# An SSM convolution and a linear-attention block: single named PSUM banks, 512-column pieces and 32-row tiles

## The chip, the cores and the metric

The kernel runs on one core of a Trainium2 chip. The engines work side by side, each through its own queue in order: PE (TensorE: matmuls, with weight loads shown as PEld), DVE (VectorE), ACT (ScalarE), POOL (GpSimd) and SP (SyncE, which here only issues DMAs). They meet through semaphores. Matmuls write PSUM, 8 banks of 512 float32 columns on 128 partitions; DVE and ACT copy results from there to SBUF. The metric is the device time of one execution in microseconds (us), lower is better.

## The reference

Two independent blocks, their outputs side by side. S = 2048 tokens, D = 576 channels, 32 heads of 18, all bf16.

```python
def _A_ref(q, k, v, shift_k, ssm_k, ssm_D):
    ...
    for t in range(ks):                                   # ks = 4
        k_shift = k_shift + k_pad[:, t:t + S, :] * shift_k[:, ks - 1 - t][None, None, :]
    kv = k_shift * v
    ...                                                   # y: causal convolution of kv with ssm_k,
    y_f = kv_f * kf_f[None, :, :, :]                      # over S, by FFTs of length 2 S
    ...
    y = y + kv * ssm_D[None, None, :]
    return q * y

def _B_ref(x, wqkv, wo):
    ...                                                   # q, k, v = x @ wqkv, per head
    phi = lambda t: jnp.where(t > 0, t + 1, jnp.exp(t)) + 1e-6
    pq, pk = phi(q), phi(k)
    kv = jnp.einsum("bhsd,bhse->bhde", pk, v)
    z = jnp.einsum("bhsd->bhd", pk)
    num = jnp.einsum("bhqd,bhde->bhqe", pq, kv)
    den = jnp.einsum("bhqd,bhd->bhq", pq, z)[..., None] + 1e-6
    o = num / den
    return (lambda x, *d: x.transpose(*d))(o, 0, 2, 1, 3).reshape(B, S, D) @ wo
```

## The kernel before

Everything is one list of small work units, `ORDER` (L30), written out by hand. A unit's name picks a function (`UNITS`, L667), its numbers are arguments, a last letter is the engine of its copy out of PSUM (A: ACT, D: DVE; P: POOL, for products and convolution steps). `tc.manual_schedule()` issues the units in that order, and each engine's queue, SP's too, takes its instructions in that order.

Block A works on channel chunks `ACH` (four of 128, then one of 64), for the input u = kv and the kernel h:
- `cv` (L413): shift convolution and product with v, in four stages of elementwise steps over [128, 16 x 128], each on DVE or POOL. The shift weights stand copied to all partitions in `Wj`, from a DMA that writes them 128 times (L338) and one ACT copy (L342). k, v, q come in by groups of chunks, `GRP`: 256, 256 and 64 channels.
- `hT` (L436): 16 PE transposes of h. `h1`/`u1` (L451): stage one of the transform, 8 matmuls of 128 columns with `G[ri]` as weights (cosines and sines, from `_dft_index`, L131, and `_sine`, L209); one call for each half `bg` and each `ri`, copied to `Ch`/`Cu`.
- `ht`/`ut` (L464): DMA transposes to `Ct`. `h2`/`u2` (L472): stage two, 8 matmuls of 512 columns on 64-row, 32-column tiles, to `T` (h) and `SU` (u).
- `pX`, `pT` (L487): the spectra's products, on DVE.
- `i1` (L497): the first inverse stage, 32 matmuls of 128 columns on two 64-row tiles with `W` as the moving operand; four calls for each 128-channel chunk (`hf`, `z`), each with a copy of 1024 columns to `V`.
- `i2` (L513): the last inverse stage with `F`, the transposes of `G` (`FT`, L524); DVE multiplies by q out of PSUM. `st` stores.

Block B:
- `xd`: x transposed by DMA. `k` (L392): one block of 128 rows, 5 matmuls of 512 and 5 of 64 columns; `q` (L401): channel groups `HCH` of 126 in pairs. Both go through `phi` (L387): exp on ACT, then min and max on DVE.
- `G` (L564): x^T pk with ones columns that carry eps, 16 matmuls of 512 and 16 of 65 columns for each block of features; DVE takes a column (`ex`), ACT adds it in its copy. `kv` (L576), `M` (L597): weights combined with the output projection. `den` (L605): denominators and reciprocals, as rows 32 j + head.
- `bc` (L630): 1/den spread to the heads' channels by a matmul with a 0/1 matrix `esel` (built on POOL at L94 and masked four times by `es` on DVE, L623), then a DVE multiply into `pqT`; 2 matmuls of 512 columns a call, 10 calls.
- `o` (L640): 10 matmuls for 128 rows, copied by ACT, stored by one DMA of 144 KB.

PSUM is a pool of four slots of two banks (L257), given out in turn to every unit.

Of the kernel before, what the change touches and what calls it, by code (L numbers as in the profile page):

```python
# [16 lines left out]
S = 2048  # L17
# [9 lines left out]
ACH = [(0, 128), (128, 128), (256, 128), (384, 128), (512, 64)]  # L27
# [3 lines left out]
wm io wu.0 ix.0 sin.1 id ix.1 hl.0 iw wk wu.40 sin.0 hT.0.D FT.1.D h1.0.0.0.A h1.0.1.0.A FT.0.D h1.0.1.1.A  # L31
h1.0.0.1.A iv sw W lw.0 xd.2 q.2.0 hc lw.1 k.8 q.2.2 q.2.1 ls Wj hl.1 hT.1.D k.9 k.11 k.10 h1.1.1.0.D xd.0 k.3
kl.0 cv.0.0.D one h1.1.0.0.A k.1 ht.0.0 h2.0.0.0.A h2.0.0.1.A eps cv.0.1.DD cv.0.2.DD q.0.1 h1.1.1.1.A q.0.0
h1.1.0.1.A xd.3 q.3.0 q.0.2 vl.0 cv.0.3.PDD k.2 cv.1.0.P k.0 ht.0.1 h2.0.1.1.A q.3.1 k.12 u1.0.1.1.A k.15
h2.0.1.0.D ht.1.1 h2.1.1.0.A k.13 u1.0.0.1.A hl.2 hT.2.D u1.0.0.0.A cv.1.1.PD k.14 xd.1 u1.0.1.0.A xl.2
cv.1.2.DD cv.1.3.DPP ht.1.0 xl.1 h2.1.1.1.A q.1.1 h2.1.0.1.A h2.1.0.0.A q.1.0 q.1.2 h1.2.1.0.A ut.0.1 k.7
u2.0.1.0.D u2.0.1.1.A k.6 h1.2.0.1.A k.4 ut.0.0 u2.0.0.1.D u2.0.0.0.A k.5 pX.0.0 pT.0.0 u1.1.1.0.A u1.1.1.1.A
q.3.2 u1.1.0.1.A xl.0 xl.3 kl.1 pX.0.1 pT.0.1 u1.1.0.0.A es G.0 vl.1 h1.2.0.0.A h1.2.1.1.A cv.2.0.D cv.2.1.DD
cv.2.2.DD G.2 ut.1.0 G.4 u2.1.0.1.D u2.1.0.0.A ut.1.1 i1.0.0.1.A hl.3 i1.0.0.0.A i1.0.1.1.A i1.0.1.0.A
cv.2.3.DDD ql.0 cv.3.0.D cv.3.1.DD u2.1.1.1.A ht.2.0 u2.1.1.0.A pX.1.1 pT.1.1 hT.3.A G.1 lwv pX.1.0 pT.1.0  # L40
h2.2.0.1.A ht.2.1 G.3 cv.3.2.DD u1.2.0.0.A i2.0.0 kl.2 u1.2.1.1.A u1.2.1.0.A kv u1.2.0.1.A i2.0.1 h2.2.0.0.A
h2.2.1.0.A den h2.2.1.1.A i1.1.1.0.A lwo M.0 i1.1.0.1.A i1.1.0.0.A i1.1.1.1.D ut.2.0 u2.2.0.0.A M.2 ut.2.1
# [23 lines left out]
def _warm(tc, psum, K, n):  # L66

    nc = tc.nc
    zero = K.sm[:, 1984:2048].bitcast(BF)
    if n:  # L70
        ps = psum.tile([128, 128], FP32, name="warm_ps", tag="big")
        for _ in range(n):
            nc.tensor.matmul(ps[:], lhsT=zero, rhs=zero, start=True, stop=True)
    else:
        nc.vector.memset(zero, 0.0)


def _head_consts(tc, cpool, K):
# [23 lines left out]
    K.jmask = cpool.tile([128, 4], FP32, name="jmask")  # L102
    nc.gpsimd.memset(K.jmask[:], 0.0)
    for j in range(4):
        nc.gpsimd.memset(K.jmask[32 * j:32 * (j + 1), j:j + 1], 1.0)
# [6 lines left out]
def _small(tc, cpool, slot, K):  # L112
# [9 lines left out]
    nc.vector.memset(K.negpi[:], -math.pi)  # L122
    K.warm = cpool.tile([128, 1], FP32, name="warm")
# [7 lines left out]
def _dft_index(tc, slot, K, part):  # L131

    nc = tc.nc
    if part == 0:
        kap = K.sm[:, 128:256].unsqueeze(1).to_broadcast([128, 16, 128])
        sv = K.sm[:, 256:272].unsqueeze(2).to_broadcast([128, 16, 128])
        K.mp = slot([128, 16, 128], I32, "mp")
        nc.vector.tensor_tensor(out=K.mp[:], in0=kap, in1=sv, op=ALU.mult)  # L138
        nc.vector.tensor_single_scalar(out=K.mp[:], in_=K.mp[:], scalar=8191, op=ALU.bitwise_and)  # L139
    else:  # L140
        K.mc = slot([128, 2, 16, 128], I16, "mc")
        nc.vector.tensor_single_scalar(out=K.mc[:, 0], in_=K.mp[:], scalar=6144, op=ALU.add)
        nc.vector.tensor_single_scalar(out=K.mc[:, 1], in_=K.mc[:, 0], scalar=8191, op=ALU.bitwise_and)


def _w16_index(tc, K):
# [21 lines left out]
    iota(sm[:, 384:448], [[1, 16], [0, 4]])  # L168
    for c, shift, mask in ((6, 1, 127), (8, 0, 1)):
# [6 lines left out]
    K.ta = sm[:, 9:10]  # L176


def _w16_phase(tc, K):
# [3 lines left out]
    K.wi = sm[:, 1536:1984].bitcast(I32)  # L183
    for i, c in enumerate((12, 8, 4, 0, 16, 12)):
        nc.gpsimd.tensor_scalar(out=K.wi[:, 64 + 64 * i:128 + 64 * i], in0=sm[:, 384:448], scalar1=prow,
                                scalar2=float(c), op0=ALU.mult, op1=ALU.add)
# [6 lines left out]
def _w16_mask(tc, K):  # L193
# [5 lines left out]
    K.wz = K.sm[:, 1152:1536]  # L199
    nc.gpsimd.memset(K.wz, 1.0 / S)  # L200
    for p in (0, 64):
        m = K.wz[p:p + 64].rearrange("p (y z) -> p y z", z=4)
        nc.gpsimd.affine_select(out=m, in_=m, compare_op=ALU.is_ge, fill=0.0, base=0, pattern=[[0, 96], [-16, 4]],
                                channel_multiplier=1)
        nc.gpsimd.affine_select(out=m, in_=m, compare_op=ALU.is_ge, fill=0.0, base=15, pattern=[[0, 96], [16, 4]],
                                channel_multiplier=-1)


def _sine(tc, cpool, K, ri):  # L209
    K.G[ri] = cpool.tile([128, 16, 128], BF, name="G%d" % ri)  # L210
    src = K.mp[:] if ri else K.mc[:, 1]
    tc.nc.scalar.activation(out=K.G[ri][:], in_=src, func=ACT.Sin, scale=TWO_PI / 8192, bias=K.negpi[:])


def _sine16(tc, K):
    nc = tc.nc
    nc.scalar.activation(out=K.sm[:, 1536:1984], in_=K.wi, func=ACT.Sin, scale=TWO_PI / 16, bias=K.negpi[:])
# [3 lines left out]
def _w16(tc, cpool, K):  # L221
    nc = tc.nc
    ws = K.sm[:, 1536:1984]
# [3 lines left out]
    K.W = cpool.tile([128, 3, 128], BF, name="W16")  # L227
    nc.vector.tensor_tensor(out=K.W[:].rearrange("p m n -> p (m n)"), in0=K.wz, in1=ws[:, 64:448], op=ALU.mult)
# [3 lines left out]
def kernel(  # L232
# [24 lines left out]
    psum = ctx.enter_context(tc.tile_pool(name="psum", bufs=4, space=PSUM))  # L257
# [9 lines left out]
    def slotv(shape, dt, name):  # L267

        return c8.tile(shape, dt, name=name, tag="vq", bufs=2)
# [37 lines left out]

    def x_D(g):
# [23 lines left out]
    Wall = slotv([128, D, 4], BF, "Wall")  # L332
# [4 lines left out]
    def load_shift():  # L337
        nc.sync.dma_start(out=Wall[:].rearrange("p d j -> p (d j)"),  # L338
                            in_=A_shift_k.rearrange("d j -> (d j)").partition_broadcast(128))

    def shift_w():
        nc.scalar.activation(out=Wj[:], in_=Wall[:].rearrange("p d j -> p j d"), func=ACT.Copy)  # L342
# [6 lines left out]
    GRP = ((0, 256), (256, 256), (512, 64))  # L349

    def load_g(key, src, gi):
        d0, dn = GRP[gi]
        n = 19 if key == 'k' else 16
        if gi == 2:
            t = lpool.tile([128, n, dn], BF, name=key, tag="tail", bufs=2)
        else:
            t = (slotk if key == 'k' else slotv)([128, n, dn], BF, key)
# [11 lines left out]
    def part(key, ci):  # L369

        d0, dc = ACH[ci]
        gi = min(ci // 2, 2)
# [19 lines left out]
    def b_k(r):  # L392
        ps = psum.tile([128, 1024], FP32, name="k_ps", tag="big")
        rr = r % 4
        for n0, n1 in ((0, 512), (512, 576)):
            for t in range(5):
                nc.tensor.matmul(ps[:, n0:n1], lhsT=xT[r // 4][:, t, rr * 128:(rr + 1) * 128],  # L397
                                 rhs=wqk[:, t, D + n0:D + n1], start=(t == 0), stop=(t == 4))
        phi(ps[:, 0:D], pk[:, r, 0:D], 128)

    def b_q(g, pair):  # L401
        ps = psum.tile([128, 2, 512], FP32, name="q_ps", tag="big")
        for j, c in enumerate(pair):
            h0, hn = HCH[c]
            for t in range(5):
                nc.tensor.matmul(ps[0:hn, j, :], lhsT=wqk[:, t, h0:h0 + hn], rhs=xT[g][:, t, :],  # L406
                                 start=(t == 0), stop=(t == 4))
        n = len(pair)
        hn = HCH[pair[0]][1]
        phi(ps[0:hn, 0:n, :], pqT[0:hn, pair[0]:pair[0] + n, g * 512:(g + 1) * 512], hn)  # L410
# [25 lines left out]
    def h_T(ci, eng='D'):  # L436
# [3 lines left out]
        ps = psum.tile([128, 16, 128], BF, name="hT_ps", tag="big")  # L440
# [10 lines left out]
    def s1(ci, xf, key, bg, ri, eng='A'):  # L451
# [5 lines left out]
        ps = psum.tile([128, 8, 128], FP32, name="s1_ps", tag="big")  # L457
        for bi in range(8):
            b = 8 * bg + bi
            nc.tensor.matmul(ps[:, bi, 0:dc], lhsT=K.G[ri][:, b, :], rhs=xf(b), start=True, stop=True)  # L460
# [11 lines left out]
    def s2(ci, hf, key, x, eng='A'):  # L472
# [4 lines left out]
        Ct = s['Ct' + key, hf][:].rearrange("p (r g j) k -> p r g j k", r=2, j=2)  # L477
        ps = psum.tile([128, 2, 512], FP32, name="s2_ps", tag="big")
        for r in range(2):
            for j in range(2):  # L480
                q = 32 * (2 * r + j)
                for z in range(2):
                    nc.tensor.matmul(ps[q:q + 32, z, :], lhsT=K.W0[64 * z:64 * z + 64, x, :],  # L483
                                     rhs=Ct[64 * z:64 * z + 64, r, :, j, :], start=True, stop=True)
        evict(s[dst, hf][:, :, x, :], ps[:], eng)

    def prod(ci, hf, key):  # L487

        s = st[ci]
        t = s['T', hf]  # L490
# [234 lines left out]
```

## Time and profile before

| What | Value |
|---|---|
| Time, median of 3 runs | 172.58 us (171.72 to 172.92) |
| The profiled execution | 171.81 us, its span 170.0 us, granted clock 0.995 |
| PE busy | 159.0 us (94%), 2176 matmuls |
| DVE busy | 139.7 us (82%) |
| ACT busy | 122.8 us (72%) |
| POOL busy | 70.9 us (42%) |
| DMA | 32.58 MB, mean 192 GB/s; queue q1 at 91% of 16 engines |

The rows of groups below have the line, engine and operation, output <- inputs with shapes, and the count; behind the bar the busy time and the mean of one in ns.

```profile
L277 ACT ACTIVATE V<-i_ps 128x1024 bf16<-128x1024 f32 x14 | 13.6, 1027 | 2.8 <-PE i_ps L507 2.1 <-ACT T L277 0.7
...
L390 DVE SCALAR_TENSOR_TENSOR pqT<-pqT,q_ps 126x1024 bf16<-126x1024 bf16 x8 | 9.7, 1217 | 3.8 <-ACT pqT L389 3.8
...
L390 DVE SCALAR_TENSOR_TENSOR pqT<-pqT,q_ps 72x512 bf16<-72x512 bf16 x4 | 2.7, 676 | 0.0
...
L433 POOL TENSOR_TENSOR v<-at,v 128x2048 bf16<-128x2048 bf16 x2 | 8.1, 4067 | 0.2
```

A copy or elementwise step of 1024 columns out of PSUM takes about 1.0 us on ACT and 1.2 on DVE; a step over 2048 bf16 columns in SBUF takes 1.2 us on DVE and 4.1 on POOL. A matmul's duration on the page (216 ns for i_ps) contains its way through the array; the next one starts earlier.

### The profile page before, as it was taken

Reading aid. Unit: us, or ns where it says so; the run is one execution under the profiler, and the core shown is the slowest. Engines: PE = TensorE matmul, PEld = TensorE weight load, DVE = VectorE, ACT = ScalarE, POOL = GpSimd, SP = SyncE. Lnnn points to the kernel's source line nnn. Section 1 sums busy time; section 2 is a strip of 40 time slices with the busy share of each in tenths; the row PEclk is TensorE's granted clock in tenths of the full one; section 3 lists DMA queues with packets and bytes.
Section 4 is the critical chain, followed back from the end, with each engine's and each line's share of the span. In section 5 each row is a group of like instructions: output and inputs, shape, how many; then the busy total and the mean of one; then the engine's idle time right before and its main releaser. Section 6 shows DMA issues by size and latency. Waiting matters only on the chain.

```text
span 170.0 us, 4984 instructions
## 1 busy us (share of the span) xinstructions
PE 159.0 (94%) x2176; PEld 106.9 (63%) x2176; DVE 139.7 (82%) x159; ACT 122.8 (72%) x142; POOL 70.9 (42%) x76
## 2 busy tenths in 40 slices
PE   4779999999999799999999999999999999999990
PEld 4768566665575456565685586857856765677750
DVE  7995589998989867999599887997999777999530
ACT  3458987977788899923597477989897778784431
POOL 7998982027693397000000049999900400000000
PEclk9999999999999999999999999999999999999997
DMA  5999699799989999999998655980959957988685
GB/s 147 273 268 250 119 267 136 137 272 225 145 183 217 263 178 318 290 213 219 306 214 196 106 150 40 182 159 18 146 126 276 202 128 69 237 180 258 191 244 117
DMA packets 81704, 32.58 MB, mean 192 GB/s; under 512 B 57432, under 2 KB 80978, under 8 KB 81682
## 3 DMA queue, kind: packets, MB, share of 16 engines
q1 hardware_dynamic: 81682, 32.26, 91.0%
q8 instruction: 17, 0.28, 0.7%
q14 instruction: 5, 0.04, 0.1%
HBM read 15.48 MB, written 4.72 MB: 119 GB/s over the span
## 4 chain that ended last, share of the span: by engine, by line
PE 77%; DMA 11%; DVE 6%; ACT 3%; issue 0%; ACTq 0%
PE q_ps L406 12%; PE g_ps L570 12%; PE k_ps L397 11%; PE o_ps L644 10%; PE s_ps L460 8%; PE i_ps L507 8%; DMA Ctu<-Cu 7%; PE s_ps L483 5%; DMA Cth<-Ch 4%; PE hT_ps L443 2%; PE i_ps L520 2%; PE i_ps L521 2%; PE bc_ps L635 1%; PE kv_ps L583 1%; DVE mp L138 1%; DVE mp L139 1%
## 5 line engine op out<-in xcount | busy, mean ns | idle before, releaser
L429 POOL TENSOR_TENSOR at<-k,Wj 128x2048 bf16<-128x2048 bf16 (+1 forms) x5 | 16.4, 3289 | 36.3 <-DVE at L430 36.2
L406 PE MATMUL q_ps<-xT,wqk 128*126 128x512 bf16 (+1 forms) x100 | 23.3, 381 | 0.0
L644 PE MATMUL o_ps<-wo_M,pqT 126*128 126x512 bf16 (+3 forms) x160 | 21.9, 286 | 0.0
L397 PE MATMUL k_ps<-wqk,xT 128*128 128x512 bf16 (+1 forms) x160 | 21.8, 286 | 0.0
L460 PEld LDWEIGHTS <-G 128*128 128x128 bf16 x320 | 17.6, 98 | 5.2 <-issue 2.1
L570 PE MATMUL g_ps<-pk,x_sb 128*128 128x512 bf16 (+3 forms) x160 | 20.4, 286 | 0.0
L277 ACT ACTIVATE Cu<-s_ps 128x1024 bf16<-128x1024 f32 (+1 forms) x18 | 16.6, 951 | 2.8 <-PE s_ps L460 2.4
L397 PEld LDWEIGHTS <-xT 128*128 128x128 bf16 x160 | 11.4, 98 | 11.1 <-issue 1.1
L644 PEld LDWEIGHTS <-pqT 126*128 126x128 bf16 (+1 forms) x160 | 11.2, 97 | 10.7 <-issue 0.8
L406 PEld LDWEIGHTS <-wqk 128*126 128x126 bf16 (+1 forms) x100 | 12.5, 131 | 8.2 <-issue 1.2
L277 ACT ACTIVATE Ch<-s_ps 128x1024 bf16<-128x1024 f32 (+1 forms) x18 | 16.3, 952 | 1.4 <-PE s_ps L460 0.8
L507 PE MATMUL i_ps<-W,T 64*128 64x128 bf16 x288 | 16.6, 216 | 0.4 <-DVE pqT L638 0.4
L649 ACT ACTIVATE ob<-o_ps 128x576 bf16<-128x576 f32 x16 | 10.4, 653 | 8.9 <-PE o_ps L644 8.7
L570 PEld LDWEIGHTS <-x_sb 128*128 128x128 bf16 (+1 forms) x160 | 10.8, 101 | 9.5 <-issue 0.2
L507 PE MATMUL i_ps<-W,X 64*128 64x128 bf16 x288 | 16.5, 216 | 0.0
L277 ACT ACTIVATE T<-s_ps 128x1024 bf16<-128x1024 f32 x16 | 15.8, 1021 | 0.6 <-PE s_ps L483 0.6
L277 ACT ACTIVATE V<-i_ps 128x1024 bf16<-128x1024 f32 x14 | 13.6, 1027 | 2.8 <-PE i_ps L507 2.1
L390 DVE SCALAR_TENSOR_TENSOR pqT<-pqT,q_ps 126x1024 bf16<-126x1024 bf16 (+1 forms) x12 | 12.2, 1037 | 3.8 <-ACT pqT L389 3.8
L522 DVE TENSOR_TENSOR q<-i_ps,q 128x1024 bf16<-128x1024 f32 (+1 forms) x10 | 11.2, 1116 | 4.6 <-PE i_ps L521 4.6
L389 ACT ACTIVATE pqT<-q_ps,neg 126x1024 bf16<-126x1024 f32 (+1 forms) x12 | 11.6, 968 | 4.3 <-PE q_ps L406 4.3
L430 POOL TENSOR_TENSOR at<-at 128x2048 bf16<-128x2048 bf16 (+1 forms) x4 | 12.4, 3094 | 5.4 <-DVE at L429 5.2
L433 POOL TENSOR_TENSOR v<-at,v 128x2048 bf16<-128x2048 bf16 (+1 forms) x3 | 10.3, 3419 | 9.8 <-DVE at L430 9.6
(120 smaller groups left out, 335.4 us busy)
## 6 DMA issues: line engine op xcount, KB each, us to landing
x_sb<-in_B_x_dram SPq DMA_DIRECT2D x4, 576.0 KB
out_dram<-ob SPq DMA_DIRECT2D x16, 144.0 KB, 4.0
h_sb<-in_A_ssm_k_dram SPq DMA_DIRECT2D x4, 512.0 KB
k<-in_A_k_dram SPq DMA_DIRECT2D x2, 1024.0 KB, 9.1
v<-in_A_v_dram SPq DMA_DIRECT2D x2, 1024.0 KB, 6.6
q<-in_A_q_dram SPq DMA_DIRECT2D x2, 1024.0 KB
out_dram<-q SPq DMA_DIRECT2D x2, 1024.0 KB
wqk<-in_B_wqkv_dram SPq DMA_DIRECT2D x2, 576.0 KB
```

The costliest lines, as they stand in the source:

```text
L277: nc.scalar.activation(out=out, in_=in_, func=ACT.Copy)
L389: nc.scalar.activation(out=out_ap, in_=ps_ap, func=ACT.Exp, bias=K.neg1[0:n, :])
L390: nc.vector.scalar_tensor_tensor(out=out_ap, in0=out_ap, scalar=1.0, in1=ps_ap, op0=ALU.min, op1=ALU.max)
L397: nc.tensor.matmul(ps[:, n0:n1], lhsT=xT[r // 4][:, t, rr * 128:(rr + 1) * 128], rhs=wqk[:, t, D + n0:D + n1], start=(t == 0), stop=(t == 4))
L406: nc.tensor.matmul(ps[0:hn, j, :], lhsT=wqk[:, t, h0:h0 + hn], rhs=xT[g][:, t, :], start=(t == 0), stop=(t == 4))
L429: on[0].tensor_tensor(out=t_, in0=kk[:, 3 - stage:19 - stage], in1=wb(stage), op=ALU.mult)
L430: on[1].tensor_tensor(out=a_, in0=a_, in1=t_, op=ALU.add)
L460: nc.tensor.matmul(ps[:, bi, 0:dc], lhsT=K.G[ri][:, b, :], rhs=xf(b), start=True, stop=True)
L507: nc.tensor.matmul(ps[:, r, g, :], lhsT=s[key, hf][64 * r:64 * r + 64, z, x, 128 * g:128 * g + 128], rhs=K.W[64 * r:64 * r + 64, m, :], st ...
L522: nc.vector.tensor_tensor(out=qs, in0=ps[:, :, 0:dc], in1=qs, op=ALU.mult)
L570: nc.tensor.matmul(ps[0:fn, n0:n1], lhsT=x_sb[:, r, f0:f0 + fn], rhs=pk[:, r, n0:n1], start=(r == 0), stop=(r == 15))
L644: nc.tensor.matmul(ps[:, n0:n1], lhsT=pqT[0:hn, c, r * 128:(r + 1) * 128], rhs=B['M'][0:hn, c, n0:n1], start=(c == 0), stop=(c == 4))
```

## The change

- PSUM: one tile over all 8 banks; each unit names its first bank(s) behind `@` in the order, a bank or a pair for each tile that it takes.
- q, k, G and the output take 512 columns in one bank; the columns behind 512 are done apart, for four row blocks at once (`kt`, `ot`) or all (`Gt`); q is done by single channel groups. Output rows are stored two blocks at a time (`os`), and may be copied by DVE.
- `i1` becomes two calls for each (`ci`, `hf`), `i1` and `j1`, each with 64 matmuls of 64 columns on four 32-row tiles with a bank for each; the copies come behind `j1`. Stage one reads its moving operand, and stage two its rows, in another order.
- `bc`: one call for each channel group, four matmuls on 32-row tiles; no `es`.
- `Wj` by matmuls with a row of ones and copies from PSUM; the cosines' index in one DVE pass; smaller masks; 1/S in the copy of `F`.
- Chunks of 128, 128, 64, 128, 128; groups of 320 and 256. Five products on POOL. Another order.

```diff
 ORDER = """
...
+io hl.0 wm wu.0 wu.40@0 ix.0 sin.1 ls id Wj.0.A@2 ix.1 sin.0 hT.0.D@4 Wj.2.D@0 iw FT.1.D@6 Wj.1.A@2 h1.0.0.1.A@4
+FT.0.D@0 hl.1 h1.0.1.0.A@2 iv h1.0.0.0.D@6 sw lw.1 wk W h1.0.1.1.D@4 xd.1 hT.1.D@0 kt.1@2 k.5@3 k.6@6 lw.0
...
+u2.3.0.0.A@6 ut.3.1 u2.3.0.1.A@2 ot.2.A@1 pX.2.0.P pT.2.0.D u1.4.0.1.A@4 o.2.D@0 ht.4.0 ot.3.D@1 u2.3.1.1.A@6
+u2.3.1.0.D@2 u1.4.1.1.A@4 pX.3.0.P pT.3.0.P o.12.D@0 i1.2.0@62 ht.4.1 u1.4.1.0.D@4 o.6.D@0 o.7.D@1 u1.4.0.0.A@4
+j1.2.0.DA@62 ot.1.D@0 os.1 os.3 pX.3.1.P h2.4.1.1.A@4 h2.4.1.0.A@6 h2.4.0.0.D@2 o.8.D@0 h2.4.0.1.A@4 i1.3.0@26
+i2.2.0@0 i2.2.1@4 j1.3.0.AA@26 ut.4.0 o.1.D@0 o.0.A@1 u2.4.0.1.D@4 u2.4.0.0.A@2 pX.4.0.D pT.3.1.P pT.4.0.D
+i1.3.1@60 j1.3.1.DA@60 ut.4.1 u2.4.1.1.A@4 o.5.A@2 o.14.D@0 i1.4.0@42 u2.4.1.0.A@6 pX.4.1.D j1.4.0.AA@42
+pT.4.1.D ql.1 o.9.A@0 i2.3.0@6 os.2 o.13.A@1 i1.4.1@42 j1.4.1.AD@42 os.0 st.0 os.6 o.15.A@0 os.7 i2.4.0@6 os.4
+st.1 i2.3.1@4 i2.4.1@2 st.2 o.11.A@0 o.10.D@1 os.5
 """
...
-        nc.vector.tensor_single_scalar(out=K.mp[:], in_=K.mp[:], scalar=8191, op=ALU.bitwise_and)
+        nc.vector.tensor_scalar(out=K.mp[:], in0=K.mp[:], scalar1=19, scalar2=19, op0=ALU.logical_shift_left,
+                                op1=ALU.arith_shift_right)
...
-        nc.vector.tensor_single_scalar(out=K.mc[:, 0], in_=K.mp[:], scalar=6144, op=ALU.add)
-        nc.vector.tensor_single_scalar(out=K.mc[:, 1], in_=K.mc[:, 0], scalar=8191, op=ALU.bitwise_and)
+        nc.vector.scalar_tensor_tensor(out=K.mc[:], in0=K.mp[:], scalar=-1.0, in1=K.mp[:], op0=ALU.mult, op1=ALU.max)
...
-    psum = ctx.enter_context(tc.tile_pool(name="psum", bufs=4, space=PSUM))
+    psum = ctx.enter_context(tc.tile_pool(name="psum", bufs=1, space=PSUM))
+    banks = psum.tile([128, 4096], FP32, name="banks")
+    taken = []
+    def pt(shape, dt=FP32):
+        b = 512 * taken.pop(0)
+        n = math.prod(shape[1:])
+        ap = banks[:, b:b + (n if dt == FP32 else n // 2)]
...
+    def b_kt(g):
+        ps = pt([128, 4, 64])
+        for r in range(4):
             for t in range(5):
+                nc.tensor.matmul(ps[:, r, :], lhsT=xT[g][:, t, r * 128:(r + 1) * 128],
+                                 rhs=wqk[:, t, D + 512:D + 576], start=(t == 0), stop=(t == 4))
+        phi(ps, pk[:, 4 * g:4 * g + 4, 512:576], 128)
...
-            nc.tensor.matmul(ps[:, bi, 0:dc], lhsT=K.G[ri][:, b, :], rhs=xf(b), start=True, stop=True)
+            nc.tensor.matmul(ps[:, bi, 0:dc].rearrange("p (z h y) -> p z h y", z=2, y=8), lhsT=K.G[ri][:, b, :],
+                             rhs=xf(b).rearrange("p (h z y) -> p z h y", z=2, y=8), start=True, stop=True)
...
+    def i1(ci, hf, z):
+        s = st[ci]
+        if z == 0:
+            s['ps', hf] = [pt([128, 2, 2, 4, 64]) for _ in range(2)]
+        ps = s['ps', hf]
+        for g in range(4):
+            for n, (key, x, m) in enumerate((('T', 0, 0), ('T', 1, 1), ('X', 0, 2), ('X', 1, 2))):
+                for r in range(2):
+                    for j in range(2):
+                        q = 32 * (2 * r + j)
+                        nc.tensor.matmul(ps[r][:, j, z, g, :], lhsT=s[key, hf][q:q + 32, z, x, 128 * g:128 * g + 128],
+                                         rhs=K.W[q:q + 32, m, :], start=(n == 0), stop=(n == 3))
+    def j1(ci, hf, eng='AA'):
+        i1(ci, hf, 1)
...
+        for r in range(2):
+            d = 64 * hf + 32 * r
+            evict(V[:, :, d:d + 32].rearrange("p j (c t) -> p c j t", t=2),
+                  s['ps', hf][r][:].rearrange("p j z g (n t) -> p (j z g) n t", t=2), eng[r])
...
+    def b_bc(c):
         h0, hn = HCH[c]
+        ps = [pt([128, 1024]) for _ in range(2)]
         for jj in range(2):
+            for gg in range(2):
+                j = 2 * gg + jj
+                nc.tensor.matmul(ps[gg][0:hn, jj * 512:(jj + 1) * 512], lhsT=K.esel[32 * j:32 * j + 32, c, 0:hn],
+                                 rhs=B['rden'][32 * j:32 * j + 32, :], start=True, stop=True)
...
+    def b_out(r, eng='A'):
+        ps = pt([128, 512])
+        for c, (h0, hn) in enumerate(HCH):
+            nc.tensor.matmul(ps, lhsT=pqT[0:hn, c, r * 128:(r + 1) * 128], rhs=B['M'][0:hn, c, 0:512],
+                             start=(c == 0), stop=(c == 4))
+        evict(ob()[:, r, 0:512], ps, eng)
...
+    def store_B(p):
+        nc.sync.dma_start(out=outB[:, 2 * p:2 * p + 2, D:2 * D], in_=ob()[:, 2 * p:2 * p + 2, 0:D])
```

284 lines of the change are left out of this document (143 added, 141 removed).

## The prediction

> **What bounds the kernel now.** I read the page's sums first, then the busy time by stretches, the list of waits for TensorE, and the chain in order of time. The stretches are cut at my own stage borders (start; forward transforms, q and k; from the first inverse stage to the last matmul; tail). Columns: window, its length, then busy time of PE, PEld, DVE, ACT, POOL, the granted clock, DMA share, GB/s.
>
> ```profile
> 0.00:15.30 15.30, 10.74 (x121) 10.35 (x122) 12.94 (x19) 7.51 (x7) 13.60 (x33) 1.00 0.95 243
> 15.30:83.60 68.30, 67.43 (x633) 40.31 (x632) 58.00 (x69) 52.58 (x61) 32.36 (x34) 1.00 1.06 215
> 83.60:165.40 81.80, 80.50 (x1431) 56.03 (x1424) 68.79 (x73) 62.03 (x75) 24.90 (x9) 1.00 0.82 167
> 165.40:170.00 4.60, 0.35 (x6) 0.19 (x4) 0.00 (x0) 0.65 (x1) 0.00 (x0) 0.81 0.56 120
> ```
>
> From 15.3 to 165.4 PE is busy 147.9 of 150.1 us, at full clock. The wait list for PE holds six entries, the longest 2.4 us at the very start, the others at most 1.2. So the matmuls themselves are the bound, and only what shortens PE's queue, the start or the tail can move the time much. DVE is second: 84% of the third stretch (68.79 of 81.80).
>
> Since a matmul's own duration contains its pipeline, I price by pitch: pieces of the chain that follow each other without a gap (start, us, what).
>
> ```profile
> 14.52 0.89 PE s_ps L460 x16
> 22.06 0.99 PE hT_ps L443 x16
> 33.37 2.16 PE q_ps L406 x10
> 39.23 2.45 PE k_ps L397 x20
> 83.65 3.68 PE i_ps L507 x128
> 104.19 1.19 PE den_ps L610 x19
> 105.38 0.11 PE den_ps L614 x19
> 117.80 0.57 PE bc_ps L635 x2
> ```
>
> 512 columns: 2.16/10 = 0.216 us. A k row block is five of 512 and five of 64: (2.45/2 - 5 x 0.216)/5 = 0.029 us for 64 columns, though each has fresh weights of 128 columns. 128 columns: 0.89/16 = 0.056. i_ps (L507) runs 128-column matmuls as pairs on two 64-row tiles: 3.68/128 = 28.8 ns each, so a pair costs what one does. den_ps puts four 32-column tiles in the array: 20 matmuls of 512 columns in some 1.1 us are five passes, and its 19 one-column matmuls start 6 ns apart.
>
> The timeline of PE shows what changing the tile shape costs:
>
> ```profile
> 106.45 0.28 PE L507 MATMUL i_ps<-W,T 64*128 64x128 bf16 x4
> 106.56 0.28 PE L507 MATMUL i_ps<-W,X 64*128 64x128 bf16 x4
> 106.76 0.43 PE L601 MATMUL m_ps<-wo_M 126*126 126x512 bf16 x1
> ```
>
> Four i_ps take 0.11, yet the full-height matmul behind the last four starts 0.20 later: about 0.095 us for the switch.
>
> **The change, part by part** (times on the span of 170.0; the profiled execution took 171.81, so 1.8 lies around the span, and it stands 0.77 under the median 172.58).
>
> Inverse stage. Now: 576 matmuls x 28.8 ns = 16.6 us. After: 1152 of 64 columns on four 32-row tiles with four banks. Four at a time they are 288 passes x 0.029 = 8.4 us: **-8.2**. The trace has no four row tiles at once. Bounds: they only pair, 576 x 0.029 = 16.7 (0), or run singly, 1152 x 0.029 = 33.4 (+16.8). I take four together: pairs by rows (i_ps) and fours by columns (den_ps) both run as one pass.
>
> 1/den broadcast. The chain has pairs at 0.44 to 0.57 us, so 20 matmuls are about 4.7. After: five passes of four, 5 x 0.22 = 1.1, and a gap or two: **-3.4** (bounds -2.2 as pairs, -3.8).
>
> Tile-shape switches. Along PE's queue the shape changes 51 times before and 71 after (the inverse stage is now cut into a first and a second half with other work between, and the broadcast is of the row-tiled shape): 20 x 0.095 = **+1.9**.
>
> q, k, G, output split into 512 columns and tails: the same matmuls in another order, 0 on PE. Stage one reads its moving operand in runs of 8: taken as 0; the nearest row with a broken-up operand, hT_ps, has 62 ns against 56, which over 320 matmuls would be +1.9. Stage two reads 512 in one run: 0, at most a small gain.
>
> Start. DVE's two passes for `mc` (1.30 + 1.58, L142 and L143) become one; the only DVE passes over 2048 int32 or f32 take 1.30 to 2.22, and a two-input one (L138) 2.22, so G[0] comes 0.7 earlier (to 1.6). One stage-one call (0.45) runs before G[0] instead of behind it. Wj's five matmuls (4 x 0.216 + 0.1 = 1.0) fall in PE's wait for G[0] (nothing of it shows if that wait stays). Together **-1.2**. On SP's queue the second h load (0.5 MB) now stands ahead of the first weights and x, while the 576 KB broadcast of the shift weights is gone: x for the first k block may come from 1 us sooner to 2 us later; taken as 0.
>
> Elementwise engines. DVE: q in 20 pieces of 0.676 (+1.1), k in 16 of 0.676 and 4 of 256 columns (0.41 by the slope between 0.676 and 1.217; +0.5), 10 output copies of 0.69 and 3 of 0.41 (+8.1), stage-one copies, of h three full and two half ones more, of u half a one more (+5.5), `mc` and `esel` (-2.2), five products to POOL (-6.1), convolution (-0.5), SU, V and hT copies (-4.3): +2.1, to about 142. ACT: its output copies leave, q, hT and k grow, 122.8 to about 119. POOL: five products of 4.06, nine instead of eight full convolution steps, no 8.8 us of mask building: 70.9 to about 84. None of it is on the path by itself. But the third stretch shrinks by 9.7 (8.2 + 3.4 - 1.9) to 72.1, and DVE's work in it, counted along the new order, grows 1.5 to 70.3: 97%. What is late next is DVE: banks wait for its reads (i2's product with q, the broadcast's multiply, output copies), and PE waits for banks. For single 10 us windows the trace has DVE at 95 to 98% with PE full (9.86 of 10 from 70 to 80), not for 70 us. At 94% the stretch is 70.3/0.94 = 74.8: **+2.7** (bounds 0; at today's 84% 83.7, +11.6).
>
> Banks by name. Four rotating slots of two banks become eight banks, so one-bank results no longer hold two. Gain: at most the 2.2 us that PE idles between 15.3 and 165.4, already low; taken as 0 beside the DVE wait.
>
> Tail. The last store now holds two row blocks (288 KB, not 144), and half of the last q group is issued just before it; output stores took 2.5 to 5.6 us to land. **+0.5** (0 to 1.5).
>
> Sum: 170.0 - 8.2 - 3.4 + 1.9 - 1.2 + 2.7 + 0.5 = 162.3; with 1.8 around it 164.1. Predicted: 164.
>
> **The rivals.**
>
> A. The order hides DVE's load: without the 2.7, with the larger gain at the start and an unchanged tail, 160. For it: those 95 to 98% windows. Against: 70 us of it. 13%.
>
> B. DVE becomes the bound at its present share of the last stage: +11.6 in place of +2.7, 173. For it: ten output copies moved to DVE, all of them late. Against: POOL takes five products, and ACT has room. 6%.
>
> C. Row tiles only pair (two at a time, as L507 shows): inverse stage 16.7, broadcast 2.2; the wait for DVE goes: 164 + 8.3 + 1.1 - 2.7 = 171. The change would then do nothing where it does most. 4%.
>
> D. The other side: slower. Each weight load of 128 columns takes its own slot of 29 ns, one after another whichever rows it goes to. Today's stage looks just the same under that rule (28.8 ns per load), and twice the loads would cost 33.4 us instead of 8.4, with no wait for DVE: 164 + 25 - 2.7 = 186. It decides as soon as four loads take over 0.1 us, since then the stage is no shorter than now. Against it: the 19 loads and matmuls of L614 in 0.11 us, though with 32 columns each. 5%.
>
> [...]
>
> E. POOL is late. The last inverse call of the fourth chunk waits for a chain of eleven POOL steps of 4.06 us (44.7 us: the last chunk's convolution, then five products); PE's own work over the same piece of the order is about 47. If the chain starts 5 us behind, PE waits and the tail follows: 168. For it: the chain starts only when DVE has done two steps of that convolution. 7%.
>
> **How the numbers follow.** The forecast has 65%, its own range 161 to 167 (the waits between 0 and +5, the start +-1.5). Low end 159.5 (A), high end 171: it takes in E and C, and leaves out B, D and the fringe, under 2 in 10. About 1% (1.7 us) is what a measurement can tell. Faster: forecast, A, E, 0.85; same: B and C, 0.10; slower: D, 0.05.
>
> **What would show it.** Right: the inverse matmuls starting in fours with about 29 ns between groups, 64 of them in about 0.47 us; the broadcast's four in 0.22; G[0] before 12 us; PE idle of 4 to 6 us behind the first inverse stage, most of it put down to DVE; POOL's last product done before the call that reads it. Wrong: 64 inverse matmuls in 0.9 us (C) or 1.8 (D); stage one at 62 ns; DVE over 96% (A) or PE idle of ten and more (B); a long wait for POOL late (E).

## The result and the profile after

| | before | after |
|---|---|---|
| median, same chip | 172.15 us (171.59 to 172.92, 4 runs) | 187.34 us (184.86 to 187.78, 4 runs) |
| ratio | | 1.083, 95% interval 1.071 to 1.095 |
| profiled execution, span, granted clock | 171.81, 170.0, 0.995 | 187.35, 185.6, 0.932 |

The change made the kernel 8% slower. Runs of one kernel spread by some per cent: ratios compare the fast runs alone, and where no ratio stands, the range of all runs stands with the median.

The busy sums hide how it came: PE 162.6 us (88% of the span, 94% before), DVE 149.7 (81%, 82% before). Two rows of the page's 40 slices, and the row of the queue that brings instructions, show more (in PEclk, 9 is full clock, 5 is half; before, that row was 9 up to the last slice, and q8 had 17 packets, 0.28 MB):

```profile
PE   4999999999879999999993996898999892996790
PEclk9999999999999999999999699558999999589788
...
q8 instruction: 21, 0.34, 0.7%
```

Busy time by stretches, cut at the same places as before (first k block; first inverse matmul; last matmul), with the same columns:

```profile
0.00:14.50 14.50, 11.80 (x141) 10.27 (x142) 12.83 (x25) 9.15 (x9) 11.47 (x29) 1.00 0.86 234
14.50:79.70 65.20, 63.58 (x641) 37.14 (x640) 61.70 (x80) 49.55 (x69) 34.82 (x27) 1.00 0.99 198
79.70:181.20 101.50, 87.19 (x1981) 56.51 (x1980) 74.68 (x76) 60.49 (x69) 49.59 (x16) 0.88 0.67 147
181.20:185.60 4.40, 0.00 (x0) 0.00 (x0) 0.47 (x1) 0.00 (x0) 0.00 (x0) 0.86 0.62 186
```

The start is 0.8 us shorter. So is the second stretch, by 3.1, but 16 of G's matmuls of 512 columns (16 x 0.216 = 3.5 us) now stand behind its end, so nothing is won there. The third, where 9.7 us were to be won, is 19.7 longer, some 3 of them that moved work: PE idles 14.3 us of it, its clock is 0.88, and no engine is full (DVE 74%). The list of waits for PE (line, what ended the wait, us, times, longest):

```profile
PE banks L550 <- issue: 3.6, 3, 2.5
PE banks L500 <- DVE hT L488: 3.2, 1, 3.2
...
PE banks L524 <- ACT V L293: 2.3, 1, 2.3
```

None of the three was there before. Yet single pieces of the chain have the pitches that were forecast:

```profile
15.25 2.16 PE banks L432 x10
23.69 0.45 PE banks L500 x8
79.97 0.66 PE banks L550 x62
```

0.216 us for 512 columns, 0.056 in stage one with its broken-up operand, and some 0.5 us for 64 inverse matmuls, about 7 ns each (L550; the rest of the 0.66 is the change of tile shape in front).

**Three places where it went.** First, the addition of one row in `h_T` (L488, two SBUF operands), DVE above, GpSimd (POOL) below:

```profile
98.23 3.79 DVE L488 TENSOR_TENSOR hT<-hT,Drow 1x128 bf16<-1x128 bf16 x1 [0.48 <-ACT hT L293]
...
97.90 4.05 POOL L470 TENSOR_TENSOR at<-at 128x2048 bf16<-128x2048 bf16 x1 [13.01 <-DVE at L469]
```

128 elements take 3.79 us, and end 0.08 us behind GpSimd's step, a sum of the convolution. Two more of the five additions were held: at 47.46 for 3.68 us (64 elements), behind which PE (L449) waits 1.2 us for DVE's next step, and at 113.57 for 0.89. Before, the addition (L448) never took over 0.43: GpSimd ran such steps then too, and two additions fell beside one, but only some 0.3 us before its end. Second, a stop inside the inverse stage:

```profile
169.75 0.24 PE L550 MATMUL banks<-W,T 32*128 32x64 bf16 x7
172.53 0.18 PE L550 MATMUL banks<-W,T 32*128 32x64 bf16 x1 [2.54 <-issue]
```

Both belong to one call, whose data have long been there; the matmul that comes late has no semaphore before it ("issue"). There are three such stops, at 85.9, 144.6 and 169.8, of 0.65, 0.76 and 2.74 us from start to start. Counted along PE's queue from 0, loads and matmuls, the instruction behind each is number 1980, 4028 and 5308: all leave 188 when divided by 256. A packet of q8 carries 16 KB, and there is one for each 256 of PE's loads and matmuls: 17 packets for 4352 before, 21 for 5514 now. The block before the longest stop began at 165.7 (instruction 5052); the packet of the next one started only at 170.1, behind a store of 1280 KB (L735, issued at 164.30, just after two of 288 KB) that kept the DMA engines full (last but one column):

```profile
165.70:170.10 4.40, 4.29 (x149) 2.75 (x137) 3.49 (x3) 3.76 (x5) 0.00 (x0) 1.00 1.03 310
```

Third, the clock, in windows around the three longest stops:

```profile
99.00:102.45 3.45, 0.37 (x7) 0.37 (x7) 3.45 (x4) 0.00 (x0) 3.37 (x2) 1.00 0.50 180
102.45:105.90 3.45, 3.45 (x43) 2.42 (x40) 2.08 (x9) 1.81 (x2) 3.45 (x1) 0.51 0.00 0
...
153.70:157.10 3.40, 0.82 (x16) 0.32 (x17) 1.23 (x1) 1.56 (x2) 0.19 (x1) 1.00 1.13 289
157.10:160.50 3.40, 2.71 (x137) 2.05 (x137) 1.54 (x2) 2.34 (x4) 0.00 (x0) 0.50 0.50 122
...
170.70:174.10 3.40, 1.57 (x46) 0.78 (x45) 0.91 (x1) 1.02 (x1) 0.00 (x0) 1.00 0.29 97
174.10:177.50 3.40, 3.13 (x30) 3.03 (x30) 1.42 (x2) 0.62 (x2) 0.00 (x0) 0.51 0.49 173
```

The windows in which PE (first sum) was busy 0.37 to 1.57 of 3.4 us still had their full clock, and the next one was granted half: matmuls of 512 columns (L708, from 160.78) then follow each other in 427 ns instead of 216. A fourth such stretch, 116.1 to 126.3, follows a window that was busy 1.73. The clock was at half for 24 us before the tail, which costs PE up to 12.

### The profile page after: what moved, and what is told of

Same layout as the page of the kernel before. It is cut to its first block, busy times and chain, and to the rows that moved or that the text cites. A ratio compares the mean times of both kernels' runs of the same rounds, so it can differ in the third digit from the quotient of the medians.

```text
span 185.6 us, 6201 instructions
## 1 busy us (share of the span) xinstructions
PE 162.6 (88%) x2757; PEld 103.9 (56%) x2757; DVE 149.7 (81%) x179; ACT 119.2 (64%) x145; POOL 95.9 (52%) x71
## 4 chain that ended last, share of the span: by engine, by line
PE 63%; DVE 21%; ACT 6%; issue 4%; DMA 3%; DVEq 0%; ACTq 0%
PE banks L449 9%; PE banks L708 9%; PE banks L432 8%; PE banks L500 7%; PE banks L550 6%; PE banks L636 6%; PE banks L524 5%; DVE hT L488 5%; PE banks L571 3%; DMA Ctu<-Cu 3%; PE banks L572 3%; PE banks L78 2%; ACT hT L293 2%; PE banks L483 2%; DVE pqT L427 2%
## 5 line engine op out<-in xcount | busy, mean ns | idle before, releaser
L449 PE MATMUL banks<-xT,wqk 128*126 128x512 bf16 (+1 forms) x100 | 24.1, 380 | 1.4 <-DVE pqT L427 1.4
L293 ACT ACTIVATE V<-banks 128x1024 bf16<-128x1024 f32 x15 | 15.2, 1062 | 13.3 <-PE banks L550 7.5
L293 ACT ACTIVATE Cu<-banks 128x1024 bf16<-128x1024 f32 (+1 forms) x18 | 16.3, 927 | 7.8 <-PE banks L500 5.3
L708 PE MATMUL banks<-wo_M,pqT 126*128 126x512 bf16 (+1 forms) x80 | 21.1, 406 | 0.0
L432 PE MATMUL banks<-wqk,xT 128*128 128x512 bf16 x80 | 19.4, 379 | 0.0
L426 ACT ACTIVATE pqT<-banks,neg 126x512 bf16<-126x512 f32 (+1 forms) x20 | 13.8, 691 | 6.9 <-PE banks L449 6.9
L636 PE MATMUL banks<-pk,x_sb 128*128 128x512 bf16 (+1 forms) x80 | 18.2, 379 | 0.0
L449 PEld LDWEIGHTS <-wqk 128*126 128x126 bf16 (+1 forms) x100 | 12.6, 131 | 9.2 <-issue 2.0
L293 ACT ACTIVATE T<-banks 128x1024 bf16<-128x1024 f32 x16 | 15.8, 1021 | 2.3 <-PE banks L524 1.8
L550 PE MATMUL banks<-W,T 32*128 32x64 bf16 x576 | 12.7, 201 | 3.8 <-issue 2.5
L293 ACT ACTIVATE SU<-banks 128x1024 bf16<-128x1024 f32 x14 | 14.0, 1021 | 2.8 <-PE banks L524 2.8
L427 DVE SCALAR_TENSOR_TENSOR pqT<-pqT,banks 126x512 bf16<-126x512 bf16 (+1 forms) x20 | 13.2, 679 | 1.0 <-ACT pqT L426 0.9
L550 PEld LDWEIGHTS <-T 32*128 32x128 bf16 x576 | 10.8, 99 | 4.8 <-issue 3.6
```

The source lines that it names most:

```text
L293: nc.scalar.activation(out=out, in_=in_, func=ACT.Copy)
L426: nc.scalar.activation(out=out_ap, in_=ps_ap, func=ACT.Exp, bias=K.neg1[0:n, :])
L427: nc.vector.scalar_tensor_tensor(out=out_ap, in0=out_ap, scalar=1.0, in1=ps_ap, op0=ALU.min, op1=ALU.max)
L432: nc.tensor.matmul(ps, lhsT=xT[r // 4][:, t, r % 4 * 128:(r % 4 + 1) * 128], rhs=wqk[:, t, D:D + 512], start=(t == 0), stop=(t == 4))
L449: nc.tensor.matmul(ps[0:hn, :], lhsT=wqk[:, t, h0:h0 + hn], rhs=xT[g][:, t, :], start=(t == 0), stop=(t == 4))
L550: nc.tensor.matmul(ps[r][:, j, z, g, :], lhsT=s[key, hf][q:q + 32, z, x, 128 * g:128 * g + 128], rhs=K.W[q:q + 32, m, :], start=(n == 0), ...
```

## The experiments

Lines are those of the kernel that was edited. The kernel before ran beside each group of kernels: 172.0 to 173.0 us, and ratios are to it.

**Undoing one suspect each, on the changed kernel.**

```diff
-        nc.vector.tensor_tensor(out=h0, in0=h0, in1=s['D'][:, 0:dc], op=ALU.add)
+        nc.vector.tensor_tensor(out=h0, in0=ps[0:1, 0, 0:dc], in1=s['D'][:, 0:dc], op=ALU.add)
```

> Kernel after, with one edit: the one-row addition behind the h transposes (L488) reads its first operand from PSUM instead of SBUF. Theory 1 (the addition, with two SBUF operands, is held while a POOL step of 4.06 us runs; PE then waits, goes idle for over 3 us and its clock is halved): all five L488 take about 0.3 us, PE's wait of 3.2 us at 98 us is gone, the clock stays full at least until 112 us, and the time falls from 187 to 176 to 181. Theory 2 (L488 is long because it waits for its DMA row or for ACT, or DVE is simply overloaded): L488 stays at 3 to 4 us and the time within 1% of 187.

Measured: 184.29 us (180.65 to 185.31), between the two theories. L488 takes 0.17 to 0.21 us, three times in the middle of a GpSimd step of 4.06, and the clock stays full until 111.3; the stop in the inverse stage stays (2.07 us, same place in the queue), and a new one comes at 45.0 (2.35 us), since chunk 2's addition now keeps a PSUM bank. The addition is one cause, worth 2 to 7 us here, not the whole.

The five products that the change gave to GpSimd, back on DVE (`pX.2.0.P` to `.D` and so on, in the order):

> Kernel after, with the five products of POOL back on DVE, nothing else. Theory 1 (POOL's late chain is a consequence and a second cost): the waits at 150 to 158 us go, L488 at 98 us stays held (that POOL step is a convolution step), 181 to 185. Theory 2 (DVE is the bound in the last stage): 6.1 us more on DVE, 188 to 193.

Measured: 190.2 us (186.8 to 195.9). The median is in the range of theory 2, but the fastest run is no slower than the changed kernel, so the time alone does not decide. With GpSimd free, PE still stops for 4.7 us at 152.6, now for a product on DVE (L537). In both kernels the chain there leads to the transposing DMA of chunk 4 (5.34 us from 150.09 in the changed one, 6.43 here), whose source buffer the V copy of ACT waits for. That the products run on GpSimd was not the cause.

The warm-up at the start shortened by 16 matmuls (`wu.40` to `wu.24`), 32 instructions:

> Kernel after with 24 warm-up matmuls instead of 40, so 32 instructions fewer ahead of everything on PE. Three stalls of after lie inside the inverse stage with no wait of any semaphore, each behind instruction 188 of a block of 256 on PE's queue. Theory 3 (they are PE waiting for its next 16 KB of instructions): the stalls stand again at the same place modulo 256, that is 16 matmuls later in the program, or where the program has long matmuls there they vanish. Rival (they are waits that the profile does not show): they stay at the same matmuls. Time within 2% of 187 either way.

Measured, in one run: 192.8 us, 3% over the changed kernel, where 2% at most was expected; here a third addition is held for over 3 us (3.85), and PE waits 3.7 us behind it. The longest stop (2.72) again stands before instruction 5308 of the queue (each load counted with its matmul, as ten matmul records are missing), which is now 16 matmuls later in the program. It belongs to a place in the instruction stream, not to a place in the work.

**The inverse stage alone, on the kernel before.**

```diff
-        ps = psum.tile([128, 2, 4, 128], FP32, name="i1_ps", tag="big")
+        ps = [psum.tile([128, 2, 2, 4, 64], FP32, name="i1_ps", tag="big") for _ in range(2)]
...
-                    nc.tensor.matmul(ps[:, r, g, :], lhsT=s[key, hf][64 * r:64 * r + 64, z, x, 128 * g:128 * g + 128],
-                                     rhs=K.W[64 * r:64 * r + 64, m, :], start=(n == 0), stop=(n == 3))
+                        for j in range(2):
+                            q = 32 * (2 * r + j)
+                            nc.tensor.matmul(ps[r][:, j, z, g, :], lhsT=s[key, hf][q:q + 32, z, x, 128 * g:128 * g + 128],
+                                             rhs=K.W[q:q + 32, m, :], start=(n == 0), stop=(n == 3))
```

(and the masks, stage one and stage two as in the change; the order and DVE's work are those of before)

> Kernel before with the 32-row inverse stage alone (its masks, stage one and two orders, both halves in one call, copies behind it); PSUM pool, order and all else as before. Theory 1 (the row tiles give what they should, the loss is in the new order with POOL and DVE): 172.2 minus about 8, 162 to 167, 128 matmuls in about 1.0 us. Theory 3 (the row tiles are the cost, by instruction supply or by shape switches): 170 or more, with stalls inside the inverse stage.

Measured: 186.47 us (183.5 to 188.3), 11 to 16 us slower where 8 were to be won. Its list of waits for PE begins:

```profile
PE i_ps L510 <- issue: 9.8, 5, 3.3
```

Nothing else of the change is in this kernel: the stops and the half clock behind them come with the row tiles. All five of these stops again stand at places of the queue that leave 188 when divided by 256.

**The supply of instructions by itself.** The kernel before, with two runs of 768 matmuls of that form on data that is there; what they write is not used.

```diff
+    def supply(n):
+        ps = [psum.tile([128, 2, 512], FP32, name="sup_ps", tag="big") for _ in range(2)]
+        for i in range(n):
+            for r in range(2):
+                for j in range(2):
+                    q = 32 * (2 * r + j)
+                    nc.tensor.matmul(ps[r][:, j, 0:64], lhsT=K.W[q:q + 32, 0, :], rhs=K.W[q:q + 32, 1, 0:64], start=True, stop=True)
```

> The kernel before with two blocks of 768 matmuls of the changed stage's form (32 rows, 64 columns, four tiles in turn, all data in place; what they write is not used), one after G of chunk 2, one after the last output matmul. Array time at 29 ns for four is 5.6 us a block. Theory A (instructions arrive in blocks of 256, slower than these use them): each block takes 7.5 to 11 us, with stops of 0.5 us or more, 256 queue rows apart and with no semaphore before them. Rival (the array sustains the rate; the changed stage waited for data): 5.6 to 6.2 us, no such stops.

Measured, in one execution: they take 21.2 and 20.6 us. Four windows of the first, columns as above:

```profile
92.27:93.94 1.67, 1.66 (x128) 1.67 (x128) 0.00 (x0) 0.00 (x0) 0.00 (x0) 0.50 0.05 10
93.94:96.00 2.06, 0.23 (x20) 0.07 (x8) 0.00 (x0) 0.00 (x0) 0.00 (x0) 0.50 0.00 0
96.00:97.67 1.67, 1.66 (x128) 1.67 (x128) 0.00 (x0) 0.00 (x0) 0.00 (x0) 0.50 0.03 10
97.67:99.73 2.06, 0.23 (x20) 0.07 (x8) 0.00 (x0) 0.00 (x0) 0.00 (x0) 0.50 0.00 0
```

128 matmuls with their 128 loads, then nothing for 2 us: 256 instructions in 3.73 us, 29.1 ns for a matmul and its load. The period before, which began at full clock and ran its 128 in 1.34 us, was 3.73 too; in the second run, the one period at full clock that is filled by such matmuls took 4.27 us, with PE busy 1.21 of them. So the array does not set it. Nor does traffic, with the DMA engines at 5% or less in the windows shown. From 88 to 100 us three packets of q8, 1.2 us each, start some 1 to 1.5 us after PE resumes, so here none started before the block ahead of it had begun. Behind the store it was worse: in the changed kernel the block begun at 165.7 was followed by the next at 172.53, 6.8 us later. So each run of 768 took two to three times what I had expected (7.5 to 11 us).

In the kernel before, the supply stayed hidden: counted in the same 256 from instruction 188, each block but the last lasted 3.69 us or more, and the list of waits for PE has no stop of this kind.

**Row tiles undone in the changed kernel**: masks, stage one, stage two and `i1` on 64 rows as before, one pair of banks for each half z; and the same with L488 reading PSUM.

```diff
-            s['ps', hf] = [pt([128, 2, 2, 4, 64]) for _ in range(2)]
-        ps = s['ps', hf]
+            s['ps', hf] = [pt([128, 2, 4, 128]) for _ in range(2)]
+        ps = s['ps', hf][z]
```

> The changed kernel with its inverse stage back on 64-row tiles (128 output columns, one pair of banks for each half z); all else as changed. Theory A1 (the starved stage is only one of three losses, beside the addition held on DVE and the late POOL chain): the three stalls (4.1 us) and the half clock behind the last (3.5 us at half, 1.7 lost) go, 8.2 us of array time come back: 186 to 192, no stall in the stage over 0.3 us. Rival A2 (the starved stage is most of the loss, as its 14 us in the kernel before would have it): 171 to 177.

> As the run with 64-row tiles, and the one-row addition of L488 also reads PSUM. A1: 3 us under the run with 64-row tiles, 182 to 189. A2: 168 to 174.

Measured: 177.95 us (ratio to before 1.029, 1.023 to 1.035) and 175.26 us (1.013, 1.006 to 1.019). No wait for instructions of over 0.2 us is left in the stage. A2 was nearly right, and my count of the stops alone (A1) far too small: with the longer stage PE no longer waits for the V copy behind the DMA of chunk 4 (2.3 us in the changed kernel), and the half clock before the tail falls from 24 to 3.4 us.

**The broadcast of 1/den alone, on the kernel before**: 32-row tiles in one call per head chunk; then in pairs, in its ten calls at their old places (this edit is shown).

```diff
-            nc.tensor.matmul(ps[0:hn, jj * 512:(jj + 1) * 512], lhsT=B['esel'][:, j, c, 0:hn], rhs=B['rden'],
-                             start=True, stop=True)
+            nc.tensor.matmul(ps[0:hn, jj * 512:(jj + 1) * 512], lhsT=K.esel[32 * j:32 * j + 32, c, 0:hn],
+                             rhs=B['rden'][32 * j:32 * j + 32, :], start=True, stop=True)
```

> The kernel before with the broadcast of 1/den alone taken from the change: 32-row tiles, one call per head chunk, the masks on DVE (L627) gone. Theory A (row tiles lose only where hundreds of short ones follow each other, because their instructions do not arrive in time): these are 20 matmuls in five calls, so nothing starves; the array gains about 3 us (15 of the 20 matmuls of 0.22 us no longer take a turn of their own), and the time is 168.5 to 171 beside 172.4. Rival B (32-row tiles lose by themselves, by switches or by their banks): 172.5 to 176.

> The kernel before with the broadcast of 1/den in 32-row tiles, but in its ten calls of two matmuls and at their old places (one PSUM buffer a call, as before); the masks on DVE gone. Theory A (the run with the broadcast alone lost by its order: calls that need two of the four buffers and two DVE products each, close together, and the half clock behind that idle time): two matmuls side by side save 10 x 0.22 = 2.2 us, 169.5 to 171.5 beside 172.5, no half clock before the tail. Rival B (the 32-row broadcast loses by itself): 173 to 178.

Measured: 178.08 us (ratio 1.027, 1.022 to 1.033) and 172.95 us (1.001, 0.996 to 1.005). Both expectations missed. In the first, five calls stand close together and each holds two of the four buffers until DVE has read them (1.2 us a product). In the 3.4 us up to 116.2 PE is busy 2.27, with waits of 0.5 us for DVE's product and 0.6 for ACT, and the clock is at half from 116.2 to 123.0; behind a wait of 1.9 us for a transposing DMA (`Ctu`) it is at half again from 143.5 to 146.9. In the second, the saving is there and is worth nothing. The stretch of the broadcast in before (first) and in this kernel:

```profile
105.00:145.00 40.00, 38.70 (x697) 26.93 (x690) 34.10 (x31) 34.47 (x43) 20.07 (x8) 1.00 0.85 142
```

```profile
105.00:145.00 40.00, 37.21 (x686) 25.48 (x675) 33.22 (x31) 33.81 (x42) 20.58 (x8) 1.00 0.86 142
```

PE is busy 1.5 us less and waits as much more: its waits of over 0.2 us there grow from 1.1 to 2.5, of them 2.0 for copies on ACT (0.7 before).

**The row-tiled calls put apart.** The kernel with the inverse stage alone in row tiles, its nine calls moved to have 2.5 us or more of longer matmuls between two (for example `i1.1.0` from behind `M.0` to behind `bc.0.1`); and that with the broadcast in pairs.

> The kernel before with the inverse stage in 32-row tiles, as in the run that did this alone (186.5 us), but its nine calls of 128 matmuls put apart in the order, with about 2.5 us or more of longer matmuls between two of them. Theory S (instructions arrive at 256 in 3.73 us, with some 160 to 220 matmuls in store; two calls in a row run dry): few stops, none over 1 us in the stage, little half clock, 164 to 169. Rival (the 32-row stage loses by itself, wherever it stands): 180 to 187.

> Both: the spread inverse stage in 32-row tiles and the broadcast in pairs. Theory S with A: 2 us under the run with the spread stage alone, 162 to 167. Rival: as it, 180 or more.

Measured: 182.7 (179.6 to 185.4) and 184.2 us (ratio 1.057, 1.049 to 1.066). Both missed: the first is better than 186.5, but four stops of 1.3 to 2.5 us remain at the ends of blocks. The longest is at 161.5, in stage i2, whose own instructions are few: the block that ended there began at 158.3 and held most of a call, and the next block's packet started only at 161.8, with the DMA engines full (share 1.07, 323 GB/s). I had put the calls apart by the rate that I measured without traffic, and by the average; this block lasted 3.2 us, and the next one came only 2.5 us after it.

**The held addition moved away by order**, on the changed kernel with 64 rows: `cv.4.1.DP` behind `hT.3.A`, `cv.1.3.PDD` to `.DDD`.

> As the changed kernel with the inverse stage on 64-row tiles (177.95 us), with two GpSimd steps moved away from the one-row addition of L488 and nothing else: the second step of chunk 4's convolution comes behind hT of chunk 3 in the order, and the third step of chunk 1's has its product on DVE. Theory (DVE's addition is held while GpSimd runs a product or a sum of two SBUF tiles): no L488 over 1.0 us, PE's gap of 2.8 us at 99.4 gone and the half clock behind it, 173.5 to 176. Rival (the addition is slow by itself or by its place in DVE's queue): L488 still over 3 us, 177 to 179.

Measured: 177.34 us (ratio 1.027, 1.020 to 1.033), no gain. The two additions are short now, but chunk 4's, 0.90 us before the edit, meets GpSimd's next step (109.00 to 113.06):

```profile
110.12 3.01 DVE L464 TENSOR_TENSOR hT<-hT,Drow 1x128 bf16<-1x128 bf16 x1 [0.16 <-ACT hT L269]
```

(the same line as L488; this kernel's order takes fewer lines). It ends with that step, PE waits 2.9 us for DVE, and the clock is at half from 114.3. So the hold came with GpSimd's step again, though it met another addition. Over the runs the addition took up to 3.85 us with two SBUF inputs (in the kernel with 24 warm-up matmuls) and at most 0.21 with one of them in PSUM (the first edit above), both beside GpSimd steps of 4.06.

**Closing the account.** No held addition, with 64-row tiles and with row tiles:

```diff
-        nc.vector.tensor_tensor(out=h0, in0=h0, in1=s['D'][:, 0:dc], op=ALU.add)
+        nc.vector.tensor_tensor(out=h0, in0=ps[0:1, 0, 0:dc] if ci > 2 else h0, in1=s['D'][:, 0:dc], op=ALU.add)
```

(and `cv.1.3.DDD`, since reading PSUM for chunk 2 had kept a bank and cost 2.4 us)

> The changed kernel with the inverse stage on 64-row tiles and no held addition: L488 reads PSUM for chunks 3 and 4 only (for chunk 2 that kept a bank and cost 2.4 us), and the third step of chunk 1's convolution has its product on DVE. If the held addition, the half clock and the starved row tiles are the whole of the cause: no PE stop over 1.2 us between 15 and 165 us, no half clock before the tail, 170 to 173, equal to the kernel before. If something else of the change costs: 175 or more.

> The same two edits on the changed kernel as it is, inverse stage in 32-row tiles. Theory S (starved instructions, and idle time behind faster stages that halves the clock): stops of 0.5 us and more at queue row 188 of 256, half clock behind them, 180 to 184, 8 us or more over the run with 64-row tiles and the same edits. Rival (row tiles only lost together with the held addition): 166 to 172, faster than the run with 64-row tiles.

Measured: 172.65 us (ratio 1.001, 0.997 to 1.005) and 180.66 us (1.047, 1.043 to 1.052), both as expected. The longest waits for PE behind the start, with 64 rows and then with row tiles:

```profile
PE banks L662 <- DVE pqT L695: 0.7, 1, 0.7
PE banks L483 <- ACT SU L293: 0.3, 1, 0.3
```

```profile
PE banks L550 <- issue: 2.8, 2, 2.5
...
PE banks L524 <- ACT V L293: 2.3, 1, 2.3
PE banks L665 <- DVE pqT L698: 0.6, 1, 0.6
```

With row tiles one stop at a block's end is still 2.5 us long, and the clock is at half from 108.5 to 118.7, 149.4 to 156.3 and 166.5 to 169.9; with 64 rows, only in the tail. The kernels differ in nothing but the row tiles (with their masks and orders), which cost 8.0 us. No version beat the kernel before.

## Why the prediction was wrong

The prediction was 164.0 us, faster; it was 187.34, slower. From its sum to the result, by the runs: 164.0, plus 16.2 for the inverse stage (8.2 not won; 8.0 lost, 180.66 - 172.65), plus 6.7 for the held additions and what follows them (187.34 - 180.66), makes 186.9; 0.4 is left for the other terms together, none of which but the broadcast was run alone.

- **Inverse stage, -8.2: the step that failed.** Its size in the array was right: the call at 79.97 ran in fours that start within 15 ns, 29 ns from one four to the next. The bounds that I set (pairs, singly) were all of the array. What failed is a cost that was not in the sum at all: the stage takes 256 instructions, 128 loads and 128 matmuls, in some 0.95 us, and their supply took 3.73 where it was measured alone. The line for it stood in the prediction: `i_ps` in 3.68 us for 128 matmuls, which are 256 instructions, just the 3.73 of the supply. By that number the stage before was already at the edge, and halving its array time could win nothing where calls follow each other. The stops are the smaller part of the loss (4.1 us in the changed kernel). The rest is the half clock behind windows in which PE had too little work: from these stops, from the wait behind the DMA of chunk 4, and around the broadcast, where PE waits for DVE and ACT. How the 8.0 us divide among these three was not measured.
- **Clock.** I priced all at full clock, since it had been full. In the changed kernel each of the four stretches at half before the tail begins behind a window of 3.41 us in which PE was busy 11 to 51%; with row tiles and no hold the three windows were busy 23 to 66%. So a stop of 3 us costs up to 1.7 us more in the window behind it (an estimate, half of 3.41), and after the window at 112.7 three in a row were at half.
- **Broadcast, -3.4.** Not on the path: as pairs in the kernel before, where 2.2 us less in the array was expected and PE was busy 1.5 less, it gave 0.1 us more (-0.6 to +0.8). In the changed kernel it was not undone by itself.
- **Held addition.** Missing. I counted what moves to GpSimd as DVE's relief (-6.1) and not what GpSimd's steps do to DVE's. The steps that held it are not the five products but convolution steps, which the new order puts beside the additions. DVE's sum, forecast at about 142 us, came to 149.7; the held additions took 7.7 us too long.
- **DVE wait, +2.7.** DVE is not the bound (74% in the stretch). With 64 rows and no hold the kernel came to 172.65, where my terms without the inverse's gain give 172.2. That is luck: the broadcast's 3.4 were not won, the 2.7 of this wait were not paid, and the two nearly cancel.
- **Switches, start, stage one.** About as priced: the full-height matmul behind the last eight of a call starts 0.18 us after them (87.12 to 87.30), of which they take 0.06, so 0.12 a switch for 0.095; the first h1 at 10.3 us, k from 14.5 instead of 15.3 us; 0.056 us a matmul in stage one.
- **Rivals.** D named the number, 29 ns for a load and matmul and 186 us, but by luck: single calls run at 7 ns a matmul with its load (64 in some 0.5 us), so the loads did not take 29 ns one after another. What took 29 ns is delivery, over a block (256 instructions in 3.73 us). A fell with the forecast. So did B, C and E: DVE is not full, row tiles do not only pair, and GpSimd's products are not what PE waits for.

What stays open: why the half clock lasts from 116.1 to 126.3, though PE was busy 3.19 and 3.07 of 3.4 us in its first two windows. Nor is the limit known: in windows of 3.41 us at full clock, from 15 us to the last matmul of the changed kernel and of the one before, PE busy 11, 24, 26, 47 or 51% was followed by half clock, and 73% or more by full. At 66% it went both ways: half with row tiles and no hold (105.1 to 108.5), full at the start of the kernel before (11.26 to 14.67). Open, too, is why the packet of a block does not start sooner.

## What to carry to other kernels

Before splitting matmuls into smaller tiles, count instructions as well as array time: here 128 matmuls with their loads took 3.7 us on quiet queues, a block of 256 instructions 6.8 beside a store of 1280 KB, and the stage, whose 128 matmuls need some 0.95 us, stopped at the block's end. A saving on a full engine counts only where that engine sets the pace; the broadcast in pairs left PE 1.5 us less to do, and the time was the same (ratio 1.001). Idle time can cost more than itself: in the changed kernel each window of 3.41 us in which PE was busy 11 to 51% was followed by half clock for 3.4 us or more. And look at what starts beside GpSimd's steps: under those of 4.06 us a one-row addition of DVE with two SBUF operands took up to 3.85 us, with one operand in PSUM at most 0.21. Let one operand come from PSUM, or keep the two apart.

## What the runs showed of the hardware

- In the kernel before and the changed one q8 moved one packet of 16 KB for each 256 of PE's loads and matmuls (17 for 4352, 21 for 5514). With the supply by itself 256 of them took 3.73 us, PE busy 1.9 of these (at half clock) and the DMA engines at 5% or less; in the changed kernel 256 took 6.8 us behind a store of 1280 KB. The three stops of the changed kernel stand each before an instruction that begins the next 256, counted from 188 (1980, 4028, 5308); with 24 warm-up matmuls the longest stands before 5308 again, 16 matmuls later in the program.
- The granted clock of the changed kernel changed at 102.46, 105.87, 116.11, 126.35, 157.07, 163.90, 174.14 and 177.55 us, whole multiples of 3.41 us apart; stretches at half lasted 3.4, 6.8 and 10.2 us.
- A DVE addition of 64 or 128 elements with two SBUF operands that started under a GpSimd sum or product of 4.06 us ended 0.04 to 0.08 us behind that step (three of five in the changed kernel), and it took up to 3.85 us in all (in the kernel with 24 warm-up matmuls); with one operand in PSUM it took 0.17 to 0.21, three times in the middle of such a step.
